# Own score blocks of a gated attention unit computed as a triangle and completed by transposes, with seven score buffers

## The chip, the cores and the metric

The kernel runs on one core of a Trainium2 chip. The metric is the device time of one execution in microseconds (us). Below, PE is TensorE, PEld its weight loads, DVE VectorE, ACT ScalarE, POOL GpSimd, SP the engine that issues most DMAs.

## The reference

Two stages follow each other. The first is an attention unit without softmax: scores of `z` with itself, ReLU, square, times `v`, gated by `u`. The second sends every token through one of eight small expert networks, chosen by a hash of its id.

```python
# u, v: (8, 2496, 256)   z: (8, 2496, 64)   w1: (8, 256, 1024)   w2: (8, 1024, 256)
scores = (1 / S) * np.matmul(z, z.transpose(0, 2, 1))
attn = np.maximum(scores, 0.0) ** 2
x = (u * np.matmul(attn, v)).reshape(B * S, D)
expert = token_ids * 2654435761 % 8
out[mask_e] = np.maximum(x[mask_e] @ w1[e], 0.0) @ w2[e]     # for each expert e
```

All data are float32. The matrix of scores is symmetric, because both its sides are the same `z`.

## The kernel before

A batch has 2496 rows: 19 tiles of 128 rows and one, number 19 (`TM`), of 64. Twenty tiles make five groups of four (`G = 4`, `NG = 5`). A group g of batch b is the set of four query tiles whose outputs are summed together in two PSUM buffers `acc`.

**Scores.** `scores(b, g)` makes, for each key tile t, one matmul of 64 rows (`K`) by up to 512 query columns. `zT` holds z transposed twice, once in each half of the partitions, and `h = ds(t % 2 * K, K)` takes the halves by turns, so that two tiles can occupy the two 64-row halves of the PE array. The result lies in one of six PSUM buffers `mm`; ACT (L188) or DVE (L186) applies the ReLU on the way to SBUF, into the block `made[b, g, t // G]` of four key tiles by 512 queries. The blocks come from `apool`, which has six buffers. `square` then squares in place, on ACT (L200) except in batch 0.

**Mirrored batches.** Batch 0 computes all scores. In batches 1 to 7 (`mirrored`), group g computes only the key tiles from its own group on, `range(g * G, T)`. The block of keys in group a < g and queries in g is the transpose of one that group a has made. DVE turns it (`turn_scores`, L215) in sixteen instructions of 32 rows, each of which transposes sixteen (or twelve) squares of 32 x 32, into one of ten buffers `m` (`mirror`). A group's own block, where key tile and query tile come from the same group, is computed in full, 4 tiles by 4 tiles.

**The order of work.** The order of each engine's instructions is the order in which the program is written (`manual_schedule`). For each group the loop does this:

1. two early steps: tiles 0 and 1 (`EARLY`), for the two halves of the queries, each followed by squares, turns and a routing step (`between`);
2. one step for each tile from 2 to 15: up to four matmuls per step (`attend`, L256), two squares, two or three turns;
3. tile 19 (`attend_last`, L250); in group 4 also the queries of the short tile (`attend_short`, L231);
4. the burst: all scores of the next group, in one row on PE;
5. the late tiles 16 to 18, again for the two halves of the queries, each followed by `gate` (DVE, L265), which multiplies `acc` by `u` and so frees it.

While group 4 runs, DVE also transposes the next batch's z (`turn_z`, L153). Ahead of the burst a loop lets enough turns go first that a free block exists. POOL writes finished rows to `x_rows` in DRAM (L449). In the last group the first expert weights and x rows are loaded; x is kept in the two `zT` buffers, and an output buffer takes one of the two `v_sb` buffers.

**Expert layers.** From about 1570 us on, `up` (L600) and `down` (L613) run over blocks of 256 tokens, with loads two blocks ahead.

Of the kernel before, what the change touches and what calls it, by code (L numbers as in the profile page):

```python
# [10 lines left out]
F32 = mybir.dt.float32  # L11
BF16 = mybir.dt.bfloat16
I32 = mybir.dt.int32
AF = mybir.ActivationFunctionType
# [10 lines left out]
def kernel(  # L25
# [10 lines left out]
    nc = tc.nc  # L36

    B, S, D = u.shape
    K = z.shape[-1]
    N = B * S  # L40
    E, _, F = moe_w1.shape
# [3 lines left out]
    P = 128  # L45
    TM = S // P
    SM = TM * P
    R = S - SM
    T = TM + 1
    assert R == 64 and K == 64  # L50
    G = 4
    NG = T // G
    assert T % G == 0
    DP = D // P
    FP = F // P
    Q = 32
    NQ = P // Q
    BLK = 256
# [6 lines left out]
    def pool(name, bufs, **kw):  # L65
        return ctx.enter_context(tc.tile_pool(name=name, bufs=bufs, **kw))
# [2 lines left out]
    mm_ps = pool("mm_ps", 6, space=bass.MemoryType.PSUM)  # L69
    acc_ps = pool("acc_ps", 2, space=bass.MemoryType.PSUM)  # L70
    npool = pool("npool", 1)
    zpool = pool("zpool", 2)
    vpool = pool("vpool", 2)
    upool = pool("upool", 2)
    apool = pool("apool", NG + 1)
    xpool = pool("xpool", 3)


# [7 lines left out]
    short = const.tile([P, T, R], F32)  # L86
# [7 lines left out]
    def width(t):  # L94
        return P if t < TM else R

    def group(g):
        return range(g * G, min(T, g * G + G))
# [16 lines left out]
    zn, zT, v_sb, u_sb, x_sb, made, mirror, to_square, to_turn, gated = {}, {}, {}, {}, {}, {}, {}, [], [], []  # L115
# [23 lines left out]
    def load_v(b):  # L139
        v_sb[b] = vpool.tile([P, T, D], F32, name="v_sb")  # L140
        for g in range(NG):
            tiles_io(vf, b, group(g), v_sb[b][:, g * G:, :], False, nc.sync, twice=True)

    def load_u(b, g):
        u_sb[b, g] = upool.tile([P, G, D], F32, name="u_sb")
        tiles_io(uf, b, group(g), u_sb[b, g], False, nc.sync)
# [13 lines left out]
    def whole(g):  # L160

        return range(G if g < NG - 1 else G - 1)
# [2 lines left out]

    def mirrored(b):
        return b > 0

    def fresh(b, g):

        return range(g * G if mirrored(b) else 0, T)

    def scores(b, g):

        n = sum(width(t) for t in group(g))
        for t in fresh(b, g):
            h = ds(t % 2 * K, K)
            ps = mm_ps.tile([P, G * P], F32, name="s_ps", tag="mm")  # L180
            nc.tensor.matmul(ps[:, 0:n], zT[b][h, ts(t, P)], zT[b][h, ds(g * G * P, n)], start=True, stop=True)  # L181
            if t % G == 0:
                made[b, g, t // G] = apool.tile([P, G, G * P], F32, name="a", tag="a")
            a = made[b, g, t // G][:, t % G, 0:n]
            if t % 4 == 3 or t % 4 == 1 and not mirrored(b):
                nc.vector.tensor_scalar_max(a, ps[:, 0:n], 0.0)  # L186
            else:
                nc.scalar.activation(a, ps[:, 0:n], AF.Relu)  # L188
            to_square.append((b, g, t))

    def square(n):
        for b, g, t in to_square[:n]:
            a = made[b, g, t // G][:, t % G, :]
            m = len(whole(g)) * P
            pairs = [(a[:, 0:m], a[:, 0:m])]
            if m < G * P:
                pairs.append((short[0:width(t), t, :], a[0:width(t), ds(m, R)]))
            for o, x in pairs:
                if mirrored(b):
                    nc.scalar.square(o, x)  # L200
                else:
                    nc.vector.tensor_mul(o, x, x)  # L202
            if mirrored(b) and t // G > g and (t % G == G - 1):
                to_turn.extend((b, g, t // G, r, c) for r in range(NQ) for c in range(NQ))
        del to_square[:n]

    def turn_scores(n):

        for b, a, g, r, c in to_turn[:n]:
            if (b, a, g) not in mirror:  # L210
                mirror[b, a, g] = mirrors.pop(0)

            m = (len(group(g)) if r * Q < width(group(g)[-1]) else G - 1) * G
            squares = "p t s q -> p (t s) q"
            nc.vector.transpose(  # L215
                mirror[b, a, g][ts(c, Q)].rearrange(squares)[:, 0:m, ts(r, Q)],
                made[b, a, g][ts(r, Q)].rearrange("p t (s q) -> p (t s) q", q=P)[:, 0:m, ts(c, Q)])
        del to_turn[:n]

    def lhs(b, g, t, i):  # L220

        if t in fresh(b, g):
            return made[b, g, t // G][:, t % G, ts(i, P)]
        return mirror[b, t // G, g][:, i, t % G, :]
# [19 lines left out]

    def attend_last(b, g, acc):

        for i in (0, 2, 1, 3):
            if i in whole(g):
                h = ds(i // 2 * R, R)
                nc.tensor.matmul(acc[i // 2][:, i % 2, :], lhs(b, g, TM, i)[h], v_sb[b][h, TM, :],  # L250
                                 start=False, stop=False, skip_group_check=True)

    def attend(b, g, t, acc, queries):
        for i in queries:
            if i in whole(g):
                nc.tensor.matmul(acc[i // 2][:, i % 2, :], lhs(b, g, t, i), v_sb[b][:, t, :],  # L256
                                 start=(t == 0 and i % 2 == 0), stop=(t == TM - 1), skip_group_check=True)

    def gate(b, g, i, acc):
        if i not in whole(g):  # L260
# [208 lines left out]
    groups = [(b, g) for b in range(B) for g in range(NG)]  # L469
    place = places()  # L470
    i = 0
# [17 lines left out]
    LOADS = 3  # L489
    w1, w2, xg, xT, hT, w_buf, xg_buf, xT_buf = {}, {}, {}, {}, {}, [], [], []  # L490
# [19 lines left out]
    def turn_x(j, k):  # L510
        xT[j] = xT_buf[k]
        nc.vector.transpose(xT[j].rearrange("p k h i -> p (k h i)"), xg[j].rearrange("p k d -> p (k d)"))

    scores(0, 0)
    square(EARLY)
    for n, (b, g) in enumerate(groups):
        if n + 1 < len(groups):
            load_u(*groups[n + 1])
        if g == 0 and b + 1 < B:
            load_z(b + 1)  # L520
            load_v(b + 1)
        if n == NG - 1:
            m = pool("mirror", 1)
            mirrors = [m.tile([P, G, G, P], F32, name=f"m_{k}") for k in range(NG * NG // 4)]

        acc = [acc_ps.tile([P, 2, D], F32, name="acc", tag="acc") for _ in range(2)]
        for k in range(2):
            for t in range(EARLY):
                attend(b, g, t, acc, [2 * k, 2 * k + 1])
            square(2)  # L530
            turn_scores(2)
            between()
        for t in range(EARLY, TM - LATE):
            if g == NG - 1 and b + 1 < B and t % 2 == 0 and t // 2 <= NG:
                turn_z(b + 1, t // 2 - 1)
            if n + 1 == len(groups) and t == T // 4:

                w_buf = list(mirrors)
                w_buf.extend(mirror[b, a, g] for a in range(NG - 1))
                load_w(0, 0)  # L540
            if n + 1 == len(groups) and t == T // 2:
                assert not gated
                xg_all, xT_all = (zpool.tile([P, T * P], F32, name="zT") for _ in range(2))
                xg_buf = [xg_all[:, ts(k, DP * BLK)].rearrange("p (k d) -> p k d", d=D // NQ) for k in range(LOADS)]
                xT_buf = [xT_all[:, ts(k, DP * BLK)].rearrange("p (k h i) -> p k h i", h=DP, i=Q) for k in range(LOADS)]
                for k in range(AHEAD):
                    load_x(k, k)
            if n + 1 == len(groups) and t >= TM - LATE - AHEAD:
                turn_x(t - (TM - LATE - AHEAD), t - (TM - LATE - AHEAD))
            attend(b, g, t, acc, range(G))  # L550
            if t % G == G - 1 and (b, t // G, g) in mirror and g < NG - 1:
                mirrors.append(mirror.pop((b, t // G, g)))
            square(2)
            turn_scores(2 + (t % 3 == 0))
            between()
        assert not to_square
        if g == NG - 1:
            gate_short(b, attend_short(b))
            if n + 1 == len(groups):
                load_w(1, 1)  # L560
            mirrors.extend(mirror.pop(k) for k in sorted(mirror))
        attend_last(b, g, acc)
        between()
        if n + 1 < len(groups):

            while len({k[:3] for k in to_turn}) + len(fresh(*groups[n + 1])) // G > NG + (g + 1 < NG):
                turn_scores(1)
            scores(*groups[n + 1])
        square(3)
        turn_scores(3)  # L570

        for k in range(2):
            for t in range(TM - LATE, TM):
                attend(b, g, t, acc, [2 * k, 2 * k + 1])
            for q in (2 * k, 2 * k + 1):
                gate(b, g, q, acc)
            square(2)
            turn_scores(2)
            between()
        between()  # L580
    assert not to_turn and next(place, None) is None and i > 2 * T + 4 * C
# [112 lines left out]
```

## Time and profile before

| | |
|---|---|
| median of 3 runs | 2701.78 us (2701.61 to 2701.83) |
| profiled execution | 2699.9 us, its span 2698.2 us |
| granted PE clock | 0.999 |
| busy share of the span | PE 99%, PEld 83%, DVE 44%, ACT 21%, POOL 18% |
| DMA | 308.87 MB, mean 114 GB/s |

A busy time is the time in which at least one instruction of the engine was running. The end of a matmul is modelled, so a busy PE doesn't mean that it works at its peak. In a row of the groups, the first number after the bar is the busy time in us, then the mean length of one instruction in ns, then the idle time ahead of it. Where instructions overlap, as score matmuls in the two halves of the array do, busy time divided by the count is less than the mean length.

The page's slices of the span show two phases: until about 1570 us DVE is busy for 0.4 to 0.8 of the time, afterwards for 0.1 to 0.2; PE is busy throughout.

### The profile page before, as it was taken

What the parts mean: (1) busy time and instruction counts of PE and PEld (TensorE: products, weight loads), DVE (VectorE), ACT (ScalarE), POOL (GpSimd) and SP (SyncE); (2) the same over time, 40 slices, a digit from 0 to 9 for tenths busy, and PEclk for the clock granted to TensorE, in tenths of its full rate; (3) what the DMA queues carried; (4) which work ended last, traced back from release to release, by engine and by line L of the source; (5) the groups of instructions that cost most, each with busy time, mean ns of one, the idle gap of its engine ahead of it and who ended that gap; (6) DMA issues with size and microseconds to landing.
All of it is one profiled execution on the core that took longest, in us unless ns stands there. A gap on an engine that the chain in (4) does not pass through costs nothing. (4 is left out here: it accounts for less than half of the span.)

```text
span 2698.2 us, 32995 instructions
## 1 busy us (share of the span) xinstructions
PE 2678.7 (99%) x12650; PEld 2248.9 (83%) x12650; DVE 1191.3 (44%) x1882; ACT 576.4 (21%) x1151; POOL 495.8 (18%) x513
## 2 busy tenths in 40 slices
PE   8999999999999999999999999999999999999998
PEld 6877887888888887887888888888888888888887
DVE  6555956847838838848758511111111111111111
ACT  2013214214223233133123111111111111111111
POOL 0221222122212221222201111111111111111113
PEclk9999999999999999999999999999999999999999
DMA  9612113013103112131001278777777778777773
GB/s 289 209 31 74 32 31 89 17 31 89 31 17 88 31 41 65 31 73 48 20 27 32 62 173 195 192 191 187 190 185 187 188 195 194 192 188 190 189 186 98
DMA packets 334835, 308.87 MB, mean 114 GB/s; under 512 B 187308, under 2 KB 293693, under 8 KB 334672
## 3 DMA queue, kind: packets, MB, share of 16 engines
q1 hardware_dynamic: 309424, 264.78, 39.4%
q0 software_dynamic: 21072, 41.10, 5.3%
q8 instruction: 102, 1.67, 0.3%
q10 hardware_dynamic: 4176, 0.82, 0.2%
q14 instruction: 61, 0.50, 0.1%
HBM read 243.25 MB, written 65.70 MB: 115 GB/s over the span
## 5 line engine op out<-in xcount | busy, mean ns | idle before, releaser
L256 PE MATMUL acc<-v_sb,a 128*128 128x256 f32 x3760 | 826.8, 380 | 1.4 <-DVE a L202 1.4
L256 PEld LDWEIGHTS acc<-v_sb,a 128*128 128x128 f32 x3760 | 710.9, 190 | 126.8 <-issue 29.0
L215 DVE STREAM_TRANSPOSE m<-a 32x512 f32<-32x512 f32 (+1 forms) x1120 | 757.1, 676 | 19.6 <-ACT a L200 2.7
L600 PE MATMUL h_ps<-zT,m 128*128 128x256 f32 x2592 | 585.3, 379 | 1.2 <-ACTq L655 1.2
L613 PE MATMUL o_ps<-m,hT 128*128 128x256 f32 x2592 | 585.2, 379 | 0.0
L600 PEld LDWEIGHTS h_ps<-zT,m 128*128 128x128 f32 x2592 | 492.4, 190 | 68.5 <-ACTq L655 1.6
L613 PEld LDWEIGHTS o_ps<-m,hT 128*128 128x128 f32 x2592 | 492.5, 190 | 67.0
L608 DVE TENSOR_SCALAR hT<-h_ps 128x512 f32<-128x512 f32 x162 | 112.1, 692 | 949.2 <-PE h_ps L600 949.2
L256 PE MATMUL acc<-v_sb,m 128*128 128x256 f32 x2016 | 439.7, 379 | 0.0
L256 PEld LDWEIGHTS acc<-v_sb,m 128*128 128x128 f32 x2016 | 383.0, 190 | 52.1
L188 ACT ACTIVATE a<-s_ps 128x512 f32<-128x512 f32 (+1 forms) x365 | 193.6, 593 | 911.9 <-PE s_ps L181 903.3
L449 POOL DMA_INDIRECT x_rows<-x_sb,slot_i x160 | 158.2, 989 | 1089.1 <-DVE x_sb L265 916.2
L625 POOL DMA_INDIRECT out_dram<-o_sb,idx x158 | 153.9, 974 | 916.5 <-ACT o_sb L620 901.4
L186 DVE TENSOR_SCALAR a<-s_ps 128x512 f32<-128x512 f32 (+1 forms) x155 | 106.1, 685 | 287.9 <-PE s_ps L181 286.8
L181 PE MATMUL s_ps<-zT 64*128 64x512 f32 (+1 forms) x1040 | 230.4, 586 | 0.0
L200 ACT ACTIVATE a<-a 128x512 f32<-128x512 f32 (+1 forms) x420 | 221.5, 624 | 0.0
L620 ACT COPY o_sb<-o_ps 128x256 f32<-128x256 f32 x162 | 60.3, 372 | 743.7 <-PE o_ps L613 743.7
L181 PEld LDWEIGHTS s_ps<-zT 64*128 64x128 f32 x1040 | 116.9, 187 | 89.1 <-issue 61.5
L437 POOL DMA_INDIRECT slot_tokens<-token,addr x160 | 159.6, 998 | 159.3 <-DVE addr L431 109.0
L606 ACT ACTIVATE hT<-h_ps 128x512 f32<-128x512 f32 x162 | 96.7, 597 | 224.8 <-PE h_ps L600 224.8
L265 DVE SCALAR_TENSOR_TENSOR x_sb<-acc,u_sb 128x256 f32<-128x256 f32 x152 | 57.8, 420 | 58.9 <-PE acc L256 58.3
L238 DVE TENSOR_TENSOR odd<-odd,q_ps 64x256 f32<-64x256 f32 x8 | 3.3, 412 | 157.3 <-ACT odd L236 157.3
(78 smaller groups left out, 352.8 us busy)
## 6 DMA issues: line engine op xcount, KB each, us to landing
m<-in_moe_w_dram SPq DMA_DIRECT2D x324, 256.0 KB, 6.7
m<-in_moe_w_dram SPq DMA_DIRECT2D x81, 1024.0 KB, 6.2
x_rows<-zero SPq DMA_DIRECT2D x10, 2176.0 KB, 16.9
zT<-x_rows SPq DMA_DIRECT2D x324, 64.0 KB, 6.1
v_sb<-in_v_dram SPq DMA_DIRECT2D x32, 512.0 KB, 5.1
u_sb<-in_u_dram SPq DMA_DIRECT2D x32, 512.0 KB, 4.0
zn<-in_z_dram SPq DMA_DIRECT2D x28, 304.0 KB, 4.7
v_sb<-in_v_dram SPq DMA_DIRECT2D x8, 384.0 KB, 7.2
```

Source lines behind the costliest of these rows:

```text
L181: nc.tensor.matmul(ps[:, 0:n], zT[b][h, ts(t, P)], zT[b][h, ds(g * G * P, n)], start=True, stop=True)
L186: nc.vector.tensor_scalar_max(a, ps[:, 0:n], 0.0)
L188: nc.scalar.activation(a, ps[:, 0:n], AF.Relu)
L200: nc.scalar.square(o, x)
L215: nc.vector.transpose(mirror[b, a, g][ts(c, Q)].rearrange(squares)[:, 0:m, ts(r, Q)], made[b, a, g][ts(r, Q)].rearrange("p t (s q) -> p (t ...
L256: nc.tensor.matmul(acc[i // 2][:, i % 2, :], lhs(b, g, t, i), v_sb[b][:, t, :], start=(t == 0 and i % 2 == 0), stop=(t == TM - 1), skip_gr ...
L437: st = nc.gpsimd.indirect_dma_start(out=slot_dram[:, None], out_offset=bass.IndirectOffsetOnAxis(ap=addr[0:n, c:c + 1], axis=0), in_=token ...
L449: st = nc.gpsimd.indirect_dma_start(out=x_dram[:, :], out_offset=bass.IndirectOffsetOnAxis(ap=slot_i[0:width(c % T), c:c + 1], axis=0), in ...
L600: nc.tensor.matmul(ps[:, i, :], w1[j][:, c, ts(f + i, P)], xT[j][:, :, c, :], start=(c == 0), stop=(c == DP - 1))
L608: nc.vector.tensor_scalar_max(o, ps[:], 0.0)
L613: nc.tensor.matmul(ps[:], hT[j][:, f, ts(t, P)], w2[j][:, f, :], start=(f == 0), stop=(f == FP - 1))
L625: st = nc.gpsimd.indirect_dma_start(out=out[:], out_offset=bass.IndirectOffsetOnAxis(ap=rows, axis=0), in_=o, in_offset=None, bounds_check ...
```

## The change

- In mirrored batches the own tile number i of a group (i = 0 to 3) is computed from column `lo` on: 128 x i in groups 2 to 4 (`fine`), 0, 0, 256, 256 in groups 0 and 1. So a key tile's scores are made for the queries of the same and later tiles alone (by pairs of tiles in groups 0 and 1). ReLU and square cover the same columns.
- DVE turns what is missing out of the same block into the same block, after squaring (`own_turns`): per 32 x 32 grid place one instruction of four squares, and in `fine` groups one more of two squares; in group 4 other cuts, which read the short tile's scores from `short`.
- The burst makes the later groups' tiles first and the own ones last, and `attend` sums in that order (`summed`). Tiles 2 and 3 of each four take the array halves in the order 1, 0 and no longer 0, 1.
- `apool` has seven buffers in place of six; `zpool` has one `zT` in place of two. The x buffers of the expert layers come from a `v_sb` buffer.
- ReLUs of mirrored batches go to ACT, but for every eighth in groups 0 and 1, which DVE does. Batch 0 still shares them evenly.
- Turns are kept in a list sorted by how soon they are wanted, own ones first. A step issues turns for 1600 units of columns, where a turn counts its columns and 170; before, it issued two or three turns. `turn_now` issues the rest of a block's turns where the block is about to be read or its buffer written anew.

```diff
-    zpool = pool("zpool", 2)
+    zpool = pool("zpool", 1)
-    apool = pool("apool", NG + 1)
+    NA = NG + 2
+    apool = pool("apool", NA)
...
     def fresh(b, g):
-        return range(g * G if mirrored(b) else 0, T)
+        if not mirrored(b):
+            return [*range(T)]
+        return [*range((g + 1) * G, T), *group(g)]
+    def summed(b, g):
+        own = group(g) if mirrored(b) else ()
+        return [t for t in range(TM) if t not in own] + [t for t in own if t < TM]
+    def skipped(b, g, t):
+        if not mirrored(b) or t // G != g:
+            return 0
+        return (t % G if fine(g) else t % G // 2 * 2) * P
+    def fine(g):
+        return g > 1
+    rooms = []
     def scores(b, g):
-        for t in fresh(b, g):
-            h = ds(t % 2 * K, K)
+        for k, t in enumerate(fresh(b, g)):
+            lo = skipped(b, g, t)
+            h = ds((t % 2 if t % G < 2 or not mirrored(b) else 1 - t % 2) * K, K)
-            nc.tensor.matmul(ps[:, 0:n], zT[b][h, ts(t, P)], zT[b][h, ds(g * G * P, n)], start=True, stop=True)
+            nc.tensor.matmul(ps[:, lo:n], zT[b][h, ts(t, P)], zT[b][h, ds(g * G * P + lo, n - lo)], start=True, stop=True)
...
-            if t % 4 == 3 or t % 4 == 1 and not mirrored(b):
+            if (k % 8 == 7 and g < 2) if mirrored(b) else k % 2:
...
+    def own_turns(b, g):
+        own = made[b, g, g]
+        tiles = own[:].rearrange("p t (i q) -> p t i q", q=P)
+        step = own[:].rearrange("p t q -> p (t q)")[:, P:G * G * P].rearrange("p (t q) -> p t q", t=G - 1)
+        def move(out, in_, n):
+            return n * Q, lambda: nc.vector.transpose(out, in_)
+        for r in range(NQ):
+            for c in range(NQ):
+                i, o = ts(r, Q), ts(c, Q)
+                if g < NG - 1:
+                    yield move(tiles[o, 2:4, 0:2, ts(r, Q)].rearrange("p s i q -> p i s q"), tiles[i, 0:2, 2:4, ts(c, Q)], 4)
+                    if fine(g):
+                        yield move(step[o, 0:3:2, ds(3 * P + r * Q, Q)], step[i, 0:3:2, ts(c, Q)], 2)
+                    continue
+                yield move(step[o, 0:2, ds(3 * P + r * Q, Q)], step[i, 0:2, ts(c, Q)], 2)
+                yield move(tiles[o, 2, 0, ts(r, Q)], tiles[i, 0, 2, ts(c, Q)], 1)
+                if c * Q < R:
+                    yield move(tiles[o, 3, 0:2, ts(r, Q)], short[i, ds(g * G, 2), ts(c, Q)], 2)
+                    yield move(tiles[ds(R + c * Q, Q), 3, 2, ts(r, Q)], short[i, g * G + 2, ts(c, Q)], 1)
+    def turn_scores(steps):
+        nonlocal turned
+        turned += steps * 1600
+        while to_turn and turned > 0:
+            n, _, f = to_turn.pop(0)
+            f()
+            turned -= n + 170
+        turned = min(turned, 0)
+    def turn_now(key):
+        for e in [e for e in to_turn if e[1] == key]:
+            to_turn.remove(e)
+            e[2]()
...
-            turn_scores(2 + (t % 3 == 0))
+            turn_scores(1)
...
-            while len({k[:3] for k in to_turn}) + len(fresh(*groups[n + 1])) // G > NG + (g + 1 < NG):
-                turn_scores(1)
+            m = len(fresh(*groups[n + 1])) // G
+            for key in rooms[max(0, len(rooms) - NA):max(0, len(rooms) - NA + m)]:
+                turn_now(key)
             scores(*groups[n + 1])
         square(3)
-        turn_scores(3)
+        turn_scores(1)
```

`attend`, `attend_last` and the late steps call `turn_now` for the block they read. The other calls of `turn_scores` become `turn_scores(1)` as well.

More of the change, by code (lines that the diff above doesn't have):

```diff
@@ L171, in fresh @@
     def fresh(b, g):
-        return range(g * G if mirrored(b) else 0, T)
+        if not mirrored(b):
[11 more added lines that the diff above has]
+    rooms = []
     def scores(b, g):
         n = sum(width(t) for t in group(g))
-        for t in fresh(b, g):
-            h = ds(t % 2 * K, K)
+        for k, t in enumerate(fresh(b, g)):
+            lo = skipped(b, g, t)
+            h = ds((t % 2 if t % G < 2 or not mirrored(b) else 1 - t % 2) * K, K)
             ps = mm_ps.tile([P, G * P], F32, name="s_ps", tag="mm")
-            nc.tensor.matmul(ps[:, 0:n], zT[b][h, ts(t, P)], zT[b][h, ds(g * G * P, n)], start=True, stop=True)
+            nc.tensor.matmul(ps[:, lo:n], zT[b][h, ts(t, P)], zT[b][h, ds(g * G * P + lo, n - lo)], start=True, stop=True)
             if t % G == 0:
                 made[b, g, t // G] = apool.tile([P, G, G * P], F32, name="a", tag="a")
-            a = made[b, g, t // G][:, t % G, 0:n]
-            if t % 4 == 3 or t % 4 == 1 and not mirrored(b):
-                nc.vector.tensor_scalar_max(a, ps[:, 0:n], 0.0)
+                rooms.append((b, g, t // G))
+            a = made[b, g, t // G][:, t % G, lo:n]
+            if (k % 8 == 7 and g < 2) if mirrored(b) else k % 2:
+                nc.vector.tensor_scalar_max(a, ps[:, lo:n], 0.0)
             else:
-                nc.scalar.activation(a, ps[:, 0:n], AF.Relu)
+                nc.scalar.activation(a, ps[:, lo:n], AF.Relu)
             to_square.append((b, g, t))
@@ L194, in square @@
             m = len(whole(g)) * P
-            pairs = [(a[:, 0:m], a[:, 0:m])]
+            lo = skipped(b, g, t)
+            pairs = [(a[:, lo:m], a[:, lo:m])] if lo < m else []
             if m < G * P:
@@ L202, in square, with turns_of, turn @@
                     nc.vector.tensor_mul(o, x, x)
-            if mirrored(b) and t // G > g and (t % G == G - 1):
-                to_turn.extend((b, g, t // G, r, c) for r in range(NQ) for c in range(NQ))
+            if mirrored(b) and t % G == G - 1:
+                turns = turns_of(b, g, t // G) if t // G > g else own_turns(b, g)
+                to_turn.extend((n, (b, g, t // G), f) for n, f in turns)
+                to_turn.sort(key=lambda e: min(e[1][2] - g, 2 if fine(g) else 1))
         del to_square[:n]
-    def turn_scores(n):
-        for b, a, g, r, c in to_turn[:n]:
+    def turns_of(b, a, g):
+        def turn(r, c, m):
@@ L210, in turn_scores @@
             if (b, a, g) not in mirror:
                 mirror[b, a, g] = mirrors.pop(0)
-            m = (len(group(g)) if r * Q < width(group(g)[-1]) else G - 1) * G
-            squares = "p t s q -> p (t s) q"
             nc.vector.transpose(
-                mirror[b, a, g][ts(c, Q)].rearrange(squares)[:, 0:m, ts(r, Q)],
+                mirror[b, a, g][ts(c, Q)].rearrange("p t s q -> p (t s) q")[:, 0:m, ts(r, Q)],
                 made[b, a, g][ts(r, Q)].rearrange("p t (s q) -> p (t s) q", q=P)[:, 0:m, ts(c, Q)])
-        del to_turn[:n]
+        for r in range(NQ):
+            for c in range(NQ):
+                m = (len(group(g)) if r * Q < width(group(g)[-1]) else G - 1) * G
+                yield m * Q, lambda r=r, c=c, m=m: turn(r, c, m)
@@ new lines, in own_turns @@
+    def own_turns(b, g):
[4 more added lines that the diff above has]
+            return n * Q, lambda: nc.vector.transpose(out, in_)
+        for r in range(NQ):
+            for c in range(NQ):
+                i, o = ts(r, Q), ts(c, Q)
[9 more added lines that the diff above has]
+                    yield move(tiles[ds(R + c * Q, Q), 3, 2, ts(r, Q)], short[i, g * G + 2, ts(c, Q)], 1)
@@ L220, in lhs @@
+    turned = 0
+    def turn_scores(steps):
[10 more added lines that the diff above has]
+            e[2]()
     def lhs(b, g, t, i):
@@ L245, in attend_last @@
     def attend_last(b, g, acc):
+        turn_now((b, TM // G, g))
         for i in (0, 2, 1, 3):
@@ L251, in attend_last, with attend @@
                                  start=False, stop=False, skip_group_check=True)
-    def attend(b, g, t, acc, queries):
+    def attend(b, g, k, acc, queries):
+        t = summed(b, g)[k]
+        turn_now((b, t // G, g))
         for i in queries:
@@ L256, in attend @@
                 nc.tensor.matmul(acc[i // 2][:, i % 2, :], lhs(b, g, t, i), v_sb[b][:, t, :],
-                                 start=(t == 0 and i % 2 == 0), stop=(t == TM - 1), skip_group_check=True)
+                                 start=(k == 0 and i % 2 == 0), stop=(k == TM - 1), skip_group_check=True)
     def gate(b, g, i, acc):
@@ L530 @@
             square(2)
-            turn_scores(2)
+            turn_scores(1)
             between()
@@ L542 @@
                 assert not gated
-                xg_all, xT_all = (zpool.tile([P, T * P], F32, name="zT") for _ in range(2))
-                xg_buf = [xg_all[:, ts(k, DP * BLK)].rearrange("p (k d) -> p k d", d=D // NQ) for k in range(LOADS)]
-                xT_buf = [xT_all[:, ts(k, DP * BLK)].rearrange("p (k h i) -> p k h i", h=DP, i=Q) for k in range(LOADS)]
+                x_all = vpool.tile([P, T, D], F32, name="v_sb")
+                x_bufs = [x_all[:, ts(k, DP * BLK // D), :].rearrange("p c d -> p (c d)") for k in range(2 * LOADS)]
+                xg_buf = [x.rearrange("p (k d) -> p k d", d=D // NQ) for x in x_bufs[:LOADS]]
+                xT_buf = [x.rearrange("p (k h i) -> p k h i", h=DP, i=Q) for x in x_bufs[LOADS:]]
                 for k in range(AHEAD):
@@ L564 @@
         if n + 1 < len(groups):
-            while len({k[:3] for k in to_turn}) + len(fresh(*groups[n + 1])) // G > NG + (g + 1 < NG):
-                turn_scores(1)
+            m = len(fresh(*groups[n + 1])) // G
+            for key in rooms[max(0, len(rooms) - NA):max(0, len(rooms) - NA + m)]:
+                turn_now(key)
             scores(*groups[n + 1])
         square(3)
-        turn_scores(3)
+        turn_scores(1)
         for k in range(2):
@@ L577 @@
             square(2)
-            turn_scores(2)
+            turn_scores(1)
             between()
```

## The prediction

> **What bounds the kernel now.** I read the page first, then busy time by stage, then the groups with shapes kept apart, then the order in time on PE and VectorE. The page gives PE 99% of the span:
>
> ```profile
> PE 2678.7 (99%) x12650; PEld 2248.9 (83%) x12650; DVE 1191.3 (44%) x1882; ACT 576.4 (21%) x1151; POOL 495.8 (18%) x513
> ```
>
> That DVE figure is an average over attention and expert layers. One batch taken by its five query groups (g = 0 to 4; us from the span's start, then busy us of PE, PEld, DVE, ACT, POOL):
>
> ```profile
> 796.90:837.90 41.00, 41.00 (x192) 33.72 (x191) 31.46 (x47) 18.25 (x36) 8.71 (x9) 1.00 0.49 121
> 837.90:878.90 41.00, 41.00 (x194) 32.81 (x196) 34.13 (x52) 14.59 (x28) 8.71 (x9) 1.00 0.09 26
> 878.90:918.10 39.20, 39.20 (x186) 31.86 (x186) 33.43 (x51) 10.94 (x21) 8.78 (x9) 1.00 0.10 28
> 918.10:955.60 37.50, 37.50 (x178) 31.07 (x178) 25.28 (x41) 7.29 (x14) 8.77 (x9) 1.00 0.09 27
> 955.60:988.20 32.60, 32.60 (x174) 26.76 (x174) 5.13 (x10) 3.63 (x11) 8.77 (x9) 1.00 0.12 33
> ```
>
> PE never idles; VectorE has 7 to 12 us of room in groups 0 to 3 and 27 us in group 4. The batch is 191.3 us. Seven batches are mirrored, so only they change. Prices, from the groups by shape (busy us, mean ns of one):
>
> ```profile
> L181 PE MATMUL s_ps<-zT 64*128 64x512 f32 x944 | 211.0, 591 | 0.0
> L215 DVE STREAM_TRANSPOSE m<-a 32x512 f32<-32x512 f32 x896 | 629.4, 702 | 16.6 <-ACT a L200 2.7
> L215 DVE STREAM_TRANSPOSE m<-a 32x384 f32<-32x384 f32 x224 | 127.8, 570 | 3.0
> ```
>
> PE's order in time where a batch's scores begin (start us, length, what):
>
> ```profile
> 796.93 0.69 PE L181 MATMUL s_ps<-zT 64*128 64x512 f32 x1
> 797.14 0.38 PE L250 MATMUL acc<-v_sb,a 64*128 64x256 f32 x1
> 797.36 8.74 PE L181 MATMUL s_ps<-zT 64*128 64x512 f32 x39
> 806.03 0.48 PE L256 MATMUL acc<-v_sb,a 128*128 128x256 f32 x1
> ```
>
> An f32 matmul is two records (passes). The 39 passes start over 806.03 - 797.36 = 8.67 us, 0.222 us each. A full-array pass of L256 has half the columns (256) and takes 826.8/3760 = 0.220 us. So two score passes run side by side, one in each 64-row half, and each half takes 0.43 us for 512 columns, 0.84 ns a column. The first two lines show that a half can overtake: a scores pass started 0.21 us ahead of an older pass of L250.
>
> [...] The two transpose rows agree: (702 - 570)/128 = 1.03 ns an element, 702 - 512 x 1.03 = 175 ns fixed.
>
> **The change part by part.**
>
> *Removed columns on PE.* A group's own four score tiles (per tile two passes) filled 4 x 0.43 = 1.72 us of each half pair. Now groups 0 and 1 keep 512, 512, 256, 256 columns, the halves taken in the order 0, 1, 1, 0: 768 per half and pass, 2 x 0.645 = 1.29 us, saved 0.43. Groups 2 and 3 keep 512 and 128 in one half, 384 and 256 in the other: 640 columns, 1.07 us, saved 0.65. The 128-column pass would take 0.107 us, but the weight load of L181 is 0.187 us long, so its two passes may last 0.37: then 1.23, saved 0.48. Group 4 (448 queries, last tile 64 columns) had 1.50 us and comes to 0.86, or by the same weight load to 1.13, saved 0.37 to 0.64. A batch: 2 x 0.43 + 2 x 0.48 + 0.37 = 2.2 us, at most 2 x 0.43 + 2 x 0.65 + 0.64 = 2.8; seven: **15 to 20 us**. I take 15.5, near the weight-load end. It is all on the path, PE being the bound.
>
> *Added turns on VectorE* (`own_turns`). By columns: 16 of 128 in groups 0 and 1; 16 of 128 and 16 of 64 in 2 and 3; 24 of 64 and 24 of 32 in 4: 144 a batch, 1008 in all. By the fit, 0.31, 0.24 and 0.21 us: 5.0, 5.0, 8.8, 8.8, 10.8, together 38.4 us a batch. This extrapolates below the smallest shape the trace has. Low end: 0.06 us of fixed part, if they overlap as L153's do (five of 128x512 in 3.08 us); high end: twice the 0.175[...]. Removed: 11 of 15 ReLUs of 0.69 (7.6 us). The old turns stay at 160 a batch but spread otherwise: in the changed instruction order 36, 41, 32, 35, 16 fall in the stretches that begin with the scores of groups 0 to 4. Stretch by stretch (0.715 a turn of 512, 0.58 of 384, gates 1.5):
> g0: 1.4 + 36 x 0.715 + 5.0 + 1.5 = 33.6 of 40.6 us;
> g1: 1.1 + 33 x 0.715 + 8 x 0.58 + 5.0 + 1.5 = 35.8 of 40.6;
> g2: 32 x 0.715 + 8.8 + 1.5 = 33.2 of 38.7;
> g3: 19 x 0.715 + 16 x 0.58 + 8.8 + 1.5 = 33.2 of 37.0;
> g4: 8 x 0.715 + 8 x 0.58 + 10.8 + 5.5 (turned z, gates, the short tile) = 26.7 of 32.2.
> Hidden behind PE's matmuls, with 3.8 us left at the least (g3). Own tiles are used last (`summed`): in group 0 they are squared some five steps into the loop and wanted nine steps of 1.76 us later, against 5 us of turning.
>
> *Gates behind turns.* VectorE runs in order, so a gate (L265) waits for turns ahead of it, and the next group's matmuls wait for the gate to free `acc`. From the end of group 3 on, the kernel before had no turn left to put in between (`m` is done, 964 on is `zT`):
>
> ```profile
> 960.86 0.76 DVE L265 SCALAR_TENSOR_TENSOR x_sb<-acc,u_sb 128x256 f32<-128x256 f32 x2 [2.13 <-PE acc L256]
> 963.45 0.76 DVE L265 SCALAR_TENSOR_TENSOR x_sb<-acc,u_sb 128x256 f32<-128x256 f32 x2 [1.83 <-PE acc L256]
> 964.12 3.08 DVE L153 STREAM_TRANSPOSE zT<-zn 128x512 f32<-128x512 f32 x5
> ```
>
> Now three turns stand between the gates where group 4 ends, where PE has little cover: three matmuls of the one query left, then four of the next group's first half, 7 x 0.44 = 3.1 us. VectorE needs about 0.2 of latency + 0.76 + 3 x 0.715 + 0.42 = 3.5. So PE waits some 0.4 to 0.5 us, seven times: 3.3 us (0 to 7). Where groups 0 to 3 end, the cover is ten matmuls, 4.4 us, against 0.2 + 0.76 + 2.15 + 0.76 = 3.9: no wait, but only 0.5 us spare.
>
> *ReLUs moved to ScalarE.* In group 0's burst of 20 it gets 18, some 0.48 us apart by its timeline for sixteen, 0.27 for two short: 8.3 us against PE's 8.3. PE may wait for a PSUM buffer by 0.2 us, seven times: 1.4 us (0 to 4).
>
> *Nothing* for the rest. One `zT` buffer: the z turns overwrite it at 964, the last scores read it by 958. Seven score buffers: no PE wait on a buffer is in the trace; they pay for holding blocks longer. The x buffers take a dead v buffer, the loads and their place in SP's queue stay. The POOL memset of the output buffer now needs the last batch's v, but POOL stood behind the last gate anyway.
>
> Sum: -15.5 + 3.3 + 1.4 = -10.8. The profiled run took 2699.9 (span 2698.2), 1.9 under the median; against the median 2701.78, **2691**, -0.4%.
>
> **Rivals.**
> *VectorE becomes the bound (slower).* If the fixed part of a small turn is 0.35 instead of 0.175, the 144 add 25 us a batch: 162 + 25 = 187 of 189, and g3 comes to 38.8 of 37.0. VectorE also idles while a burst feeds its ReLUs (1.02 us at a time in its timeline). Some 4 us over a batch, seven times, is +28: with -10.8, 2719. It decides from about 0.12 us more a turn, where g3's 3.8 us is used up; between that and the fit, the gates' 0.5 us goes first. For it: no such shape in the trace. Against: both transpose rows lie on one line, and z turns are cheaper.
> *The halves lock.* The order 0, 1, 1, 0 puts two score tiles of one half behind each other, 30 times a batch. If the other half can't overtake, each costs a weight-load stagger, which I estimate at 0.107 us (128 columns at 0.84 ns): 210 x 0.107 = 22 us, so 2713. Against: the overtaking pass. Should it cost once a burst, it is 35 x 0.107 = 4 us, 2695.
> *Gain used up.* All 28 other group ends wait 0.3 us for late gates: +8, so 2699, no change. It needs but 0.8 us more delay on VectorE.
> *It doesn't do what it says*: excluded, the built order has the shorter matmuls.
>
> **How the numbers follow.** Forecast (2682 to 2696) 0.74; VectorE bound 0.12; halves lock 0.05; gain used up 0.09. A measurement can tell 0.2%, 5.4 us: faster is below 2696.4, slower above 2707.2. Gain used up (0.09) and the near edge of VectorE's case (0.01) give "same" 0.10; the rest of VectorE's (0.11) and most of the lock's (0.04) "slower" 0.15; the forecast and a lock once a burst (0.01) "faster" 0.75. The range takes in the full column gain with no waits, 2701.8 - 19.6 = 2682, and reaches past "gain used up" to 2703, which leaves some 0.15 above it.
>
> **What would show it.** Right: L181's PE busy time down by some 15 us, own turns near 0.31, 0.24 and 0.21 us, DVE some 162 us a batch, PE idle under 1 us a batch, at the first matmuls after group 4. Wrong: own turns of 0.4 us, PE waiting for transposes in groups 1 to 3, score passes of 512 columns more than 0.43 us apart in a half.

## The result and the profile after

The changed kernel takes 2686.94 us (median of 6 runs, 2686.58 to 2688.99) against 2701.47: 0.9948 of the kernel before, 95% interval 0.9937 to 0.9958. It is 14.5 us faster; the forecast was 10.8 us.

Page of the changed kernel, busy time by engine:

```profile
PE 2662.1 (99%) x12650; PEld 2255.2 (84%) x12650; DVE 1357.5 (51%) x2813; ACT 567.6 (21%) x1221; POOL 494.2 (18%) x513
```

PE has 16.6 us less to do (2678.7 before), and is still at 99%. VectorE got 166 us more; apart from one late gate (experiment 4), none of it shows in the time.

Busy time by stage, the same batch as in the prediction, each stretch from the start of one burst of scores to the start of the next (columns: stretch, its length, then busy us of PE, PEld, DVE, ACT and POOL, the granted PE clock, and two of DMA):

```profile
790.61:832.54 41.93, 41.61 (x198) 34.37 (x197) 31.83 (x57) 18.44 (x38) 8.69 (x9) 1.00 0.48 119
832.54:873.05 40.51, 40.51 (x194) 32.93 (x192) 34.02 (x63) 14.60 (x30) 8.69 (x9) 1.00 0.09 26
873.05:911.63 38.58, 38.58 (x186) 32.19 (x184) 33.15 (x72) 10.89 (x24) 8.75 (x9) 1.00 0.09 28
911.63:948.49 36.86, 36.86 (x178) 31.34 (x176) 30.75 (x72) 6.86 (x16) 8.74 (x9) 1.00 0.10 28
948.49:980.61 32.12, 32.12 (x176) 26.83 (x173) 23.52 (x74) 3.05 (x12) 8.75 (x9) 1.00 0.11 34
```

VectorE now works through group 4 as well (23.5 us, 5.1 before). Only the first stretch has idle time on PE, 0.32 us. Cut at the same places, the kernels compare as follows (us):

| stretch from the scores of group | before | changed | difference |
|---|---|---|---|
| 0 | 41.78 | 41.93 | +0.15 |
| 1 | 40.93 | 40.51 | -0.42 |
| 2 | 39.22 | 38.58 | -0.64 |
| 3 | 37.50 | 36.86 | -0.64 |
| 4 | 32.71 | 32.12 | -0.59 |
| batch | 192.14 | 190.00 | -2.14 |

Seven batches of this length give -15.0 us. That is the whole result: in order of time, the expert layers of the changed kernel begin here (start, length), 14.9 us earlier than before (1569.99):

```profile
1555.11 10.52 PE L675 MATMUL h_ps<-v_sb,m 128*128 128x256 f32 x48
```

The span of the profiled execution fell by 13.1 us only (2698.2 to 2685.1), because its expert layers took 1.8 us longer; the medians differ by 14.5. When the changed kernel was run and profiled again (`e10_changed_again`), the expert layers took 1128.1 us, as before the change (1128.2), so the 1.8 us belong to that one execution.

### The profile page after: what moved, and what is told of

Read it like the earlier page. It is cut to its first block, busy times and chain, and to the rows that moved or that the text cites. A ratio compares the mean times of both kernels' runs of the same rounds, so it can differ in the third digit from the quotient of the medians.

```text
span 2685.1 us, 33980 instructions
## 1 busy us (share of the span) xinstructions
PE 2662.1 (99%) x12650; PEld 2255.2 (84%) x12650; DVE 1357.5 (51%) x2813; ACT 567.6 (21%) x1221; POOL 494.2 (18%) x513
## 5 line engine op out<-in xcount | busy, mean ns | idle before, releaser
L675 PE MATMUL h_ps<-v_sb,m 128*128 128x256 f32 x2592 | 586.0, 379 | 2.2 <-issue 1.1
L675 PEld LDWEIGHTS h_ps<-v_sb,m 128*128 128x128 f32 x2592 | 492.3, 190 | 70.3 <-issue 2.1
L212 ACT ACTIVATE a<-s_ps 128x512 f32<-128x512 f32 (+3 forms) x442 | 205.7, 578 | 902.9 <-PE s_ps L204 902.9
L204 PE MATMUL s_ps<-zT 64*128 64x512 f32 (+5 forms) x1040 | 211.2, 549 | 0.0
L257 DVE STREAM_TRANSPOSE a<-a 32x128 f32<-32x128 f32 (+2 forms) x896 | 201.4, 249 | 7.8
L225 ACT ACTIVATE a<-a 128x512 f32<-128x512 f32 (+3 forms) x413 | 202.1, 625 | 0.0
L204 PEld LDWEIGHTS s_ps<-zT 64*128 64x128 f32 x1040 | 123.9, 187 | 81.8 <-issue 57.2
L210 DVE TENSOR_SCALAR a<-s_ps 128x512 f32<-128x512 f32 (+1 forms) x78 | 51.4, 659 | 146.6 <-PE s_ps L204 145.5
L338 DVE SCALAR_TENSOR_TENSOR x_sb<-acc,u_sb 128x256 f32<-128x256 f32 x152 | 57.9, 420 | 133.7 <-PE acc L329 132.8
```

Source lines behind the costliest of these rows:

```text
L204: nc.tensor.matmul(ps[:, lo:n], zT[b][h, ts(t, P)], zT[b][h, ds(g * G * P + lo, n - lo)], start=True, stop=True)
L212: nc.scalar.activation(a, ps[:, lo:n], AF.Relu)
L257: return n * Q, lambda: nc.vector.transpose(out, in_)
L675: nc.tensor.matmul(ps[:, i, :], w1[j][:, c, ts(f + i, P)], xT[j][:, :, c, :], start=(c == 0), stop=(c == DP - 1))
```

## Experiments

"Changed" below is the changed kernel run again (`e10_changed_again`): 

> The changed kernel itself, for the comparison on one chip: 0.9948 of before by the earlier runs; by the theory e3 must lie 3.4 us under it, e2 4.5 us over it and e1 19 us over it.

It measured 2684.89 us, 0.9944 of before (0.9931 to 0.9958). The experiments ran on two chips: `e9` to `e12` on one, where the kernel before took 2699.9 us, and the others on another, where it took 2700.1 to 2700.2. So a difference of 0.3 us between runs on different chips means nothing. Ratios are to the kernel before on the same chip.

**1. Are the columns the gain?** (`e1_full_columns`)

```diff
 def skipped(b, g, t):
-    if not mirrored(b) or t // G != g:
-        return 0
-    return (t % G if fine(g) else t % G // 2 * 2) * P
+    return 0
```

> All columns of the own score tiles are computed again; the own turns, the seven buffers, the order of tiles and the shares of ReLU stay as in the changed kernel. Theory (PE's time for the columns is the whole gain): the 19.2 us by which L204 is shorter than L181 come back, 2686.9 + 19 = 2706, which is slower than the kernel before (2701.5) by the wait for the gate. Rival (the new order, the seven buffers or ScalarE's ReLUs bring a part): at most 2701.

Measured: 2704.11 us, 1.0015 of before (1.0009 to 1.0022), 19.2 us over the changed kernel. So the columns bring all of it, and the rest of the change, taken alone, is a loss of 4 us. In the trace that loss stands in one place: the first stretch of a batch takes 42.36 us (41.78 before), the other four take what they took before, to 0.01 us. Experiment 4 finds what it is.

**2. Are the own turns hidden?** (`e9_full_no_own_turns`: `skipped` as in 1, and)

```diff
-    return n * Q, lambda: nc.vector.transpose(out, in_)
+    return n * Q, lambda: None
```

> All columns of the own score tiles are computed, as in e1, and the own turns, which would move nothing new, are left out; their places in the list of turns are kept, so that the other turns stand where they stood. Theory (the 32 us of own turns a batch are hidden behind PE): the same as e1 within 1 us, 1.0015 of the kernel before. Rival (VectorE's added work costs PE something here and there): 3 us or more faster than e1.

Measured: 2704.22 us, 1.0016 (1.0010 to 1.0023), the same as 1. The 1008 added transposes cost nothing where they stand. (The first stretch is 42.36 us here too, so the loss of 4 us isn't theirs.)

**3. Do the halves lock?** (`e2_halves_by_turns`)

```diff
-    h = ds((t % 2 if t % G < 2 or not mirrored(b) else 1 - t % 2) * K, K)
+    h = ds(t % 2 * K, K)
```

> The array halves go 0, 1, 0, 1 again in mirrored batches, so that the own tiles of groups 2 to 4 put 768 columns (640 in group 4) in one half and 512 (384) in the other. Theory (halves run independently, the fuller one sets the time): 128 columns x 2 passes x 0.84 ns = 0.215 us more in each of groups 2, 3 and 4, 0.65 us a batch, 4.5 us in seven: 2691.5. Rival (two tiles of one half behind each other cost a stagger of 0.1 us, 30 times a batch): the order 0, 1, 0, 1 is faster, 2686.9 + 4.5 - up to 22, so 2670 to 2685.

Measured: 2689.41 us, 0.9961 (0.9948 to 0.9975), 4.5 us over the changed kernel, as the fuller half's columns give. In the trace the stretches of groups 2, 3 and 4 are longer by 0.21, 0.20 and 0.16 us. In groups 0 and 1 both orders put the same columns into each half, and there the stretches are unchanged (41.93 and 40.51 us). So the order 0, 1, 1, 0 has no price of its own.

**4. Is the idle time on PE the third gate?** (`e3_gate_first`)

```diff
             square(2)
-            turn_scores(1)
+            if k or g < NG - 1:
+                turn_scores(1)
```

> Where group 4 ends, no turns are issued between the first two gates and the third. Theory (PE's 0.48 us gap at the next group's first matmuls is the wait for that gate behind three turns): 7 x 0.48 = 3.4 us less, 2683.5. Rival (the gap is a wait for something else, or the turns are missed later): 2686.9 or more.

Measured: 2681.06 us, 0.9931 (0.9917 to 0.9944), 3.8 us under the changed kernel. What VectorE did in the changed kernel where group 4 ends, in order of time, and what PE did:

```profile
802.18 0.76 DVE L338 SCALAR_TENSOR_TENSOR x_sb<-acc,u_sb 128x256 f32<-128x256 f32 x2 [3.38 <-PE acc L329]
802.85 2.12 DVE L241 STREAM_TRANSPOSE m<-a 32x512 f32<-32x512 f32 x3
805.00 0.42 DVE L338 SCALAR_TENSOR_TENSOR x_sb<-acc,u_sb 128x256 f32<-128x256 f32 x1
...
805.48 3.72 PE L329 MATMUL acc<-v_sb,a 128*128 128x256 f32 x16 [0.32 <-issue]
```

PE restarts 0.06 us after the third gate's end (805.42), and the pass before had started 0.70 us earlier, where 0.22 is usual: 0.48 us lost. The first pass after the wait then takes 0.32 us until the next one starts, another 0.10. The same place in `e3_gate_first`:

```profile
800.05 0.76 DVE L338 SCALAR_TENSOR_TENSOR x_sb<-acc,u_sb 128x256 f32<-128x256 f32 x2 [3.38 <-PE acc L329]
801.35 0.42 DVE L338 SCALAR_TENSOR_TENSOR x_sb<-acc,u_sb 128x256 f32<-128x256 f32 x1 [0.54 <-PE acc L329]
801.69 4.98 DVE L241 STREAM_TRANSPOSE m<-a 32x512 f32<-32x512 f32 x7
```

Now the gate waits for PE and no longer PE for the gate. The first stretch of a batch falls from 41.93 to 41.35 us, which is the 0.48 and the 0.10; the others stay. Seven times 0.58 is 4.1 us, which agrees with the 3.8 and with the loss of 4 in experiment 1. The three turns in between are old ones that now stand at another place, not own turns.

**5. Do ScalarE's ReLUs cost anything?** (`e6_relu_as_before`)

```diff
-    if (k % 8 == 7 and g < 2) if mirrored(b) else k % 2:
+    if t % 4 == 3 if mirrored(b) else k % 2:
```

> ReLUs of mirrored batches are shared as before (every fourth tile on VectorE), the rest is the changed kernel. Theory (ScalarE's burst isn't the limit, and VectorE has 190 - 153 = 37 us free a batch for the 7.6 us more): within 2 us of the changed kernel, 0.9948 of before. Rival 1 (bursts waited for ScalarE): 1 to 4 us faster. Rival 2 (VectorE has no room at the gates): over 5 us slower.

Measured: 2685.63 us, 0.9946 (0.9932 to 0.9960): no difference, and all five stretches are as long as in the changed kernel. Neither engine limits a burst by its share of ReLUs.

**6. How near is VectorE to its edge?** First all own turns twice (`e4_double_own_turns`):

```diff
-    return n * Q, lambda: nc.vector.transpose(out, in_)
+    return n * Q, lambda: [nc.vector.transpose(out, in_) for _ in range(2)]
```

> Each own turn is issued twice, the second time with the same data: some 32 us more of VectorE a batch, 153 + 32 = 185 of 190. Theory (VectorE is hidden, but near its edge: with double own turns the stretches of groups 2 and 3 hold 40.2 us of work in 38.6 and 37.8 in 36.9, and VectorE also idles at every burst until the gates' matmuls are done, 3 to 5 us a time): PE waits for transposes, 50 to 150 us slower than the changed kernel. Rival (VectorE has real slack, its work spreads over the batch): under 10 us slower.

Measured: 2850.08 us, 1.0559 (1.0543 to 1.0576), 165 us slower, more than the upper end. PE's waits in it:

```profile
PE acc L329 <- DVE x_sb L338: 60.6, 33, 4.9
PE acc L321 <- DVE a L257: 30.0, 10, 5.7
PE s_ps L204 <- DVE a L210: 11.6, 7, 1.7
```

The gates (L338) come first, then the own turns themselves (L257), then ReLUs (L210). Together that is 102 us. PE also ran at a granted clock of 0.980 for 0.999, which by an estimate (0.019 of 2845.6) is another 54 us; the two experiments that follow show where it comes from. They do the same with `range(2 if g == 0 else 1)` and with `range(2 if g == 2 else 1)`:

> Own turns issued twice in group 0 alone, 5.0 us more of VectorE a batch. Theory 1 (what counts is the free time of a stretch: 41.9 - 31.8 = 10 us): nothing, within 2 us of the changed kernel. Theory 2 (what counts is the time to the next wait: turns run until 1.6 us into the burst of group 1, and VectorE then stands idle only 2.06 us before the ReLU of that burst's eighth tile): the ReLU is 5.0 - 2.1 = 3 us late, of which six PSUM buffers hide some 1.2; 1.8 us a batch, 12 us slower (5 to 20).

Measured: 2714.73 us, 1.0057 (1.0041 to 1.0072), 29.8 us slower. The stretch of group 0, which had 10 us free, didn't get longer (41.94); the next one did, from 40.51 to 44.92. Its order in time at the start of that burst:

```profile
649.34 7.18 DVE L241 STREAM_TRANSPOSE m<-a 32x512 f32<-32x512 f32 x10
...
656.55 0.69 DVE L210 TENSOR_SCALAR a<-s_ps 128x512 f32<-128x512 f32 x1
...
657.29 1.74 PE L204 MATMUL s_ps<-zT 64*128 64x512 f32 x6 [1.66 <-DVE a L210]
```

The burst starts at 649.47; ten turns, which must come before it in VectorE's order, run until 656.5, and only then VectorE's first ReLU frees its PSUM buffer. PE starts no pass from 655.04 to 657.29. After that its granted clock (third number from the end) is low for a while, and then full again:

```profile
658.96:662.00 3.04, 3.04 (x8) 2.50 (x8) 1.82 (x3) 3.02 (x8) 0.00 (x0) 0.51 0.01 3
662.00:665.00 3.00, 3.00 (x15) 2.64 (x15) 1.64 (x4) 3.00 (x7) 0.97 (x1) 1.00 0.00 0
```

In the first of these windows passes of 256 columns start 0.43 us apart where 0.22 is usual. So the 4.4 us consist of two parts: the burst takes 2.95 us longer than in the changed kernel (9.49 for 6.54), most of it the wait, and the 24 passes behind it take 1.45 us longer (6.74 for 5.29), all of it the clock (0.49 of 3.04 us is an estimate of 1.5). Free time of a stretch (theory 1) is not the measure here, time to the next wait (theory 2) is. Theory 2's place was right; its size (1.8 us a batch, 12 us in all) was too small, because the wait was longer than it said and because it had no term for what follows a wait.

> Own turns issued twice in group 2 alone, 7.1 us more of VectorE a batch. Theory 1 (free time of the stretch: 38.6 - 33.2 = 5.4 us): 1.7 us over, 12 us slower. Theory 2 (time to the next wait: the last turns of the stretch, which free blocks, already end 0.4 us into the burst of group 3, whose ReLUs write those blocks): ReLUs up to 7 us late, PE stops when six PSUM buffers are full, some 5 us a batch, 35 us slower (20 to 50).

Measured: 2717.18 us, 1.0066 (1.0051 to 1.0082), 32.3 us slower. The size is as in theory 2 (35 us), but the mechanism is another, so it was luck that the size came out right:

```profile
728.89 11.47 DVE L241 STREAM_TRANSPOSE m<-a 32x512 f32<-32x512 f32 x16
730.17 2.96 PE L204 MATMUL s_ps<-zT 64*128 64x512 f32 x16
...
740.39 0.76 DVE L338 SCALAR_TENSOR_TENSOR x_sb<-acc,u_sb 128x256 f32<-128x256 f32 x2
...
741.20 3.30 PE L329 MATMUL acc<-v_sb,m 128*128 128x256 f32 x7 [2.69 <-DVE x_sb L338]
```

The burst runs through; sixteen turns keep VectorE until 740.4, the gates behind them are late, and PE waits 2.69 us for `acc`. Again the clock falls (0.995 over the whole run, 0.999 in the changed kernel): the 96 passes from 741.20 on take 22.34 us where the changed kernel takes 20.72, 1.6 us more. Passes 0.43 us apart follow six of the seven such waits in this run, and six of seven in the run before. In the changed kernel, where PE is idle for 0.32 us before the third gate, the clock stays at 1.00 and the passes at 0.22 us. What sets the clock was not tested; that it falls after these waits is what the traces show.

**7. What is the seventh score buffer for?** (`e7_six_buffers`)

```diff
-    NA = NG + 2
+    NA = NG + 1
```

> Six score buffers in place of seven, the rest is the changed kernel. Then one more block has to be turned before each burst: (0,3) before that of group 1, in a stretch where VectorE has 41.9 - 31.8 = 10 us free and 16 turns take 11.5. Theory (the seventh buffer is what lets VectorE spread its turns): PE waits for buffers or gates at some bursts of each batch, 10 to 60 us slower than the changed kernel. Rival (the seventh buffer isn't needed): within 3 us of it.

Measured: 2748.58 us, 1.0181 (1.0165 to 1.0197), 64 us slower, just over the upper end. The loss lies in one stretch, that of group 1 (49.54 us for 40.51): before its burst a third block has to be turned, and VectorE comes to its ReLU only after that:

```profile
654.39 16.49 DVE L241 STREAM_TRANSPOSE m<-a 32x512 f32<-32x512 f32 x23
670.91 0.69 DVE L210 TENSOR_SCALAR a<-s_ps 128x512 f32<-128x512 f32 x1
671.66 2.93 PE L204 MATMUL s_ps<-zT 64*128 64x512 f32 x6 [4.84 <-DVE a L210]
```

The wait is 4.84 us; behind it the clock is 0.50 from 671.66 to 674.60, as in experiment 6.

**8. A better version** (`e8_gate_first_fine_in_0`: 4, and)

```diff
 def fine(g):
-    return g > 1
+    return g != 1
```

> e3 with the fine cut (columns from 128 x i on) in group 0 as well. PE saves 128 columns x 2 passes x 0.84 ns = 0.215 us in group 0, 1.5 us in seven batches; VectorE has 16 turns of 64 columns more there, 16 x 0.207 = 3.3 us, in a stretch with 10 us free. Theory (columns are the gain, turns are hidden while a stretch has room): 1.5 us less than e3, 0.9925 of before. Rival (the further turns make a gate late): the same as e3 or slower.

Measured: 2678.93 us, 0.9923 (0.9909 to 0.9937): the fastest of all, 6.0 us under the changed kernel and 2.1 under `e3_gate_first`. The stretch of group 0 falls from 41.35 to 41.14, the 0.21 us of the columns (1.5 us in seven batches, as expected; the rest of the 2.1 is not explained).

## Why the prediction was right

**PE is the bound and every removed column is on the path: right.** Experiment 1 gives 19.2 us for the columns, and the score passes' busy time fell by as much (L181 before, L204 after; 1040 passes for 520 score tiles in both, two a tile):

```profile
L181 PE MATMUL s_ps<-zT 64*128 64x512 f32 (+1 forms) x1040 | 230.4, 586 | 0.0
L204 PE MATMUL s_ps<-zT 64*128 64x512 f32 (+5 forms) x1040 | 211.2, 549 | 0.0
```

**The size of that term: too small, 15.5 for 19.2.** The step that failed is the choice near the weight-load end. I let a 128-column pass last as long as its weight load is recorded (0.187 us). In the changed kernel's trace the two 128-column passes of a fine group start 0.109 us apart (877.344 and 877.453 in the batch above), although the load between them is recorded with 0.187 us and as ending after the second pass began. Groups 2 and 3 so save 0.64 us and group 4 0.59, close to what the columns alone give (0.65 and 0.64). A batch saves 2.72 us by its columns (192.14 before, 189.42 in `e3_gate_first`, where the wait for the gate is gone); the prediction took 2.2 and had 2.8 as the most.

**Gates behind turns: right in place and size.** Predicted 0.4 to 0.5 us a batch where group 4 ends, with 0.2 of latency in it (before the change a gate starts 0.20 us after the start of the pass behind its last one, 963.45 for 963.25); seen 0.48, and 0.10 for the first pass after it, which the prediction had no term for. Taking the wait away brings 3.8 us (3.3 predicted for seven). No other group end waits, as forecast.

**ReLUs on ScalarE, 1.4 us: not there.** Experiment 5 shows no difference. The spacing was close to the predicted 0.48 and 0.27: in group 0's burst of the changed kernel ScalarE's ReLUs of 512 columns start 0.48 us apart where they follow each other closely, the two of 256 columns 0.26.

**The sum.** The forecast was -15.5 + 3.3 + 1.4 = -10.8. The experiments give -19.2 + 3.8 + 0 = -15.4, the stretches of the traces -19.0 + 4.1 = -14.9; the medians differ by 14.5, and by 15.0 when the changed kernel was run again. The columns (3.7 us too little gain) and the ReLUs (1.4 us too much loss) err on the same side, and only the gate, 0.5 us too small, works against them. They do not cancel: the forecast was too cautious by about 4 us, and the result lies inside its range, which took in the full gain of the columns.

**Own turns hidden, at the fitted prices: right.** By shape in the changed kernel:

```profile
L257 DVE STREAM_TRANSPOSE a<-a 32x128 f32<-32x128 f32 x448 | 135.6, 303 | 6.1
L257 DVE STREAM_TRANSPOSE a<-a 32x64 f32<-32x64 f32 x336 | 69.5, 207 | 1.6
L257 DVE STREAM_TRANSPOSE a<-a 32x32 f32<-32x32 f32 x112 | 18.1, 162 | 0.1
```

0.31, 0.24 and 0.21 us were predicted from 512 and 384 columns: right at 128, too dear below (0.207 and 0.162; the two shapes that read `short` took 0.19 and 0.20). So VectorE's sums by stretch were somewhat high: together 162.5 us a batch against 153.3 seen. That a turn's fixed part weighs most in small turns is what these rows show: a quarter of the columns (32 for 128) costs more than half the time (0.162 for 0.303 us). Experiment 2 shows the sum to be hidden.

**The rivals.** Halves that lock: refuted by 3 (the pairs in question are 25 a batch, not 30, which changes nothing in that). VectorE as the bound: not so at these prices, but nearer than I said. I put the edge at 0.12 us more a turn, from 3.8 us of free time in a stretch; experiment 6 shows that such sums don't set it. 5 us more in the stretch with the most free time (10 us) already cost 30 us, because VectorE's next obligation (a ReLU or a gate) stands behind the turns in its order. "Gain used up", with gates late from 0.8 us of delay on, was nearer to this in kind: a wait behind turns, though experiment 6 met it at other places.

## What to carry to other kernels

When PE is busy throughout, price a removed matmul column by the spacing of passes in its own array half (here 0.43 us for 512 columns), and let the fullest half decide (groups 2 and 3: 0.64 us saved, 0.65 by that price). Work moved to an in-order engine is free only until that engine's next instruction that someone waits for; look for that instruction, not for the free share of a stage (5.0 us more in a stretch with 10 us free made the next one 4.4 us longer). An urgent instruction (here a gate that frees an accumulator) goes ahead of bulk work of two microseconds (2.12 us of turns), which was worth about 4 us (3.8) for two lines. And a wait of the bounding engine can cost more than it lasts: in experiment 6, 2.69 us of waiting were followed by 1.6 us lost at a lower clock.

## What was unexpected of the hardware

A weight load recorded with 0.187 us did not keep 128-column f32 passes from starting 0.109 us apart in one half. The two 64-row halves of the array ran free of each other: with 0, 1, 1, 0 as the order of the halves, the stretches of groups 2 and 3 became shorter by 0.64 us where the fuller half's columns give 0.65, and with 0, 1, 0, 1, which puts 128 columns more into one half, longer again by 0.21 and 0.20 us (experiment 3). And after most of the waits in which PE was idle for 1.66 to 4.84 us, its granted clock fell to about half (0.51 for 3.04 us in the window shown, 0.50 for 2.94 us in experiment 7), while after the 0.32 us of the changed kernel it stayed full.
